# Layer norms with a mean taken from scaled row sums, a residual added by the matmul engine, and a new order of stages

## The chip, the cores and the metric

The kernel runs on one core of a Trainium2 chip. A core has a matmul engine (TensorE, PE in the profile), three engines for elementwise work (VectorE or DVE, ScalarE or ACT, GpSimd or POOL) and a queue that issues transfers (SyncE or SP). The metric is the device time of one execution in microseconds (us), as the median of several runs.

## What is computed

```
h   = q + q_ln * (causal_conv(kv, ssm_k) + kv * ssm_D)     # q_ln = layernorm(q), kv = shift_conv(k) * v
h2  = h + (silu(hn @ w_gate) * (hn @ w_up)) @ w_down       # hn = layernorm(h)
layernorm(x) = (x - mean(x)) / sqrt(var(x) + 1e-5)         # over the last axis, no weights
```

The sequence has 2048 rows, the model width D is 640, the width of the feed-forward part is 1728. All inputs and the output are bfloat16. The long convolution is done in the reference with Fourier transforms; the kernel does it with cosine and sine tables and matmuls.

## The kernel before

The 2048 rows are four blocks of 512 rows. For each block i the kernel runs these stages: `kv` (short convolution of k as matmuls with diagonal matrices, times v, in L551 to L561), `xfwd` (forward transform, L516, evicted by ACT in L522, combined by DVE in L504), `prod` (complex products with the transformed filter, all on DVE, L574 to L587), `ln1` (statistics of the layer norm of q), `inverse` (inverse transform on PE in L617, first residual, second layer norm, a transposing transfer of each quarter into `hnT`), and `ffn` (28 groups of gate and up matmuls in L664 and L665, ACT evictions in L680 and L682, a product on DVE in L684, 112 matmuls of the down projection in L695, the last residual in L703, the store in L706). The filter has its own stages: `ktrans`, `kfwd` and `kcomb`. `prod(i, k)` for k > i adds block i's part of the later blocks' outputs. One buffer each holds `XH`, `kT`, `vT`, `kvo` and `hnT`, so a stage of the next block waits until the last reader of the one before is through. Sixteen `gu` buffers serve the 14 products of an `ffn`, so the gate and up part of the next block can run only two groups ahead of the down projection of the block before.

A layer norm before the change takes four ScalarE passes over a quarter of a block in all: a sum, and a sum of squares of x - mean. Between the two, POOL multiplies the sum by -1/D (L594 for a whole block in `ln1`, L635 for each quarter in `inverse`). After the second, POOL scales and adds epsilon (L600, L639) and takes the power -1/2 (L602, L641), and in `ln1` also multiplies mean and reciprocal root (L604). The normalised q is made by ACT (L624) and multiplied on DVE with the matmul's result in PSUM (L628); L630 adds q. L643 normalises h.

Nothing in the order of instructions is written by hand. Each instruction is a task with a cost, a latency and a priority; `schedule` (L152) simulates the five engines and always gives a free engine the ready task with the lowest priority number, then `emit` (L239) writes one in-order stream for each engine, with semaphore waits. The table `ORDER` (L306) has a number for every engine and stage. The costs are estimates: L594 is planned with 580 ns, L600 with 600 ns, L602 with 650 ns, L604 with 600 ns. An instruction that takes longer on the chip holds up whatever the plan put behind its reader.

Of the kernel before, what the change touches and what calls it, by code (L numbers as in the profile page):

```python
# [64 lines left out]
class _Graph:  # L65
# [37 lines left out]
    def add(self, eng, fn, cost, prio, r=(), w=(), pr=(), pw=(), skip=(), lat=None, nbytes=0, after=()):  # L103
        t = _Task()
        t.eng, t.fn, t.cost, t.prio = eng, fn, cost, prio
        t.lat = lat if lat is not None else {"pe": 200, "act": 110, "dve": 110, "pool": 110, "sp": 2000}[eng]
# [208 lines left out]
    ("dve", "kv2"): 1563.9, ("dve", "kv3"): -223.1, ("dve", "mul"): -299.8, ("dve", "p00"): -640.7,  # L315
    ("dve", "p01"): 1772.6, ("dve", "p02"): 1678.0, ("dve", "p03"): 1641.2, ("dve", "p11"): -646.5,
    ("dve", "p12"): 1612.8, ("dve", "p13"): -299.8, ("dve", "p22"): -853.5, ("dve", "p23"): 1590.2,
    ("dve", "p33"): -216.0, ("dve", "res"): 1564.1, ("dve", "xf0"): -292.2, ("dve", "xf1"): -223.6,
# [13 lines left out]
def bass_sequential_preLN__ssm_conv_h3__swiglu_ffn__prompt_kernel(  # L332
# [39 lines left out]
    with ExitStack() as es:  # L372
# [24 lines left out]
        t1 = sb("t1", 131232, [2, 2, D])  # L397
        t2 = sb("t2", 136352, [2, 2, D])
# [28 lines left out]
        def cpe(n, k):  # L427
            return k * (n / 2.4 + 2.5)

        def cact(n, ptr=0):  # L430
            return 90 + 0.833 * n + 93 * ptr

        def cdve(n):
            return 75 + n / 1.92

        def cps(n):
            return (n + 80) / 0.96
# [87 lines left out]
        def kfwd(m, dst, prio):  # L525
            halves(KT[m], ktab, "kf", dst, KO, 1.0 / N, prio, prio)
# [41 lines left out]
        def prod(j, i, prio):  # L568
            cm, y = C[i - j], Y[i]
            for f2 in range(2):  # L570
# [18 lines left out]
        def ln1(i, prio):  # L589
            x, s = xh[i % 2], st1[i % 2]  # L590
            for j in range(4):
                g.add("act", lambda e, j=j: e.activation(out=qo[j][:], in_=x[:, j, :], func=ACTF.Identity, accum_out=s[:, 0, j:j + 1]),  # L592
                      cact(D, 3), prio, r=[x[:, j, :]], w=[qo[j][:], s[:, 0, j:j + 1]])
            g.add("pool", lambda e: e.tensor_scalar(out=s[:, 1, :], in0=s[:, 0, :], scalar1=-1.0 / D, scalar2=None, op0=ALU.mult), 580, prio,  # L594
                  r=[s[:, 0, :]], w=[s[:, 1, :]])
            for j in range(4):
                g.add("act", lambda e, j=j: e.activation(out=qo[j][:], in_=x[:, j, :], func=ACTF.Square, bias=s[:, 1, j:j + 1],  # L597
                                                         accum_out=s[:, 2, j:j + 1]), cact(D, 4), prio,
                      r=[x[:, j, :], s[:, 1, j:j + 1]], w=[qo[j][:], s[:, 2, j:j + 1]])
            g.add("pool", lambda e: e.tensor_scalar(out=s[:, 3, :], in0=s[:, 2, :], scalar1=1.0 / D, scalar2=LN_EPS, op0=ALU.mult,  # L600
                                                    op1=ALU.add), 600, prio, r=[s[:, 2, :]], w=[s[:, 3, :]])
            g.add("pool", lambda e: e.tensor_tensor(out=s[:, 4, :], in0=s[:, 3, :], in1=half[:, 0:4], op=ALU.pow), 650, prio,  # L602
                  r=[s[:, 3, :], half[:]], w=[s[:, 4, :]])
            g.add("pool", lambda e: e.tensor_tensor(out=s[:, 5, :], in0=s[:, 1, :], in1=s[:, 4, :], op=ALU.mult), 600, prio,  # L604
                  r=[s[:, 1, :], s[:, 4, :]], w=[s[:, 5, :]])

        def inverse(i, prio):
            for j in range(4):
# [14 lines left out]
                q = qo[j % 4]  # L623
# [161 lines left out]
```

## Time and profile before

| what | value |
|---|---|
| median of 3 runs | 312.88 us (312.87 to 313.02) |
| the profiled execution, whole time | 313.7 us |
| its span, first to last instruction | 311.9 us |
| mean granted TensorE clock in it | 0.97 of full speed |
| busy share of the span: PE, DVE, ACT, POOL | 86%, 71%, 56%, 18% |

The shares are averages over stages that differ, so the rows further down cut the span into stretches. In rows of the timeline the columns are the start, the duration, the engine, the line, the operation, what is written and read, the count, and in brackets the idle time of that engine before it and what ended it.

### The profile page before, as it was taken

Reading aid. Unit: us, or ns where it says so; the run is one execution under the profiler, and the core shown is the slowest. Engines: PE = TensorE matmul, PEld = TensorE weight load, DVE = VectorE, ACT = ScalarE, POOL = GpSimd, SP = SyncE. Lnnn points to the kernel's source line nnn. Section 1 sums busy time; section 2 is a strip of 40 time slices with the busy share of each in tenths; the row PEclk is TensorE's granted clock in tenths of the full one; section 3 lists DMA queues with packets and bytes.
Section 4 is the critical chain, followed back from the end, with each engine's and each line's share of the span. In section 5 each row is a group of like instructions: output and inputs, shape, how many; then the busy total and the mean of one; then the engine's idle time right before and its main releaser. Section 6 shows DMA issues by size and latency. Waiting matters only on the chain.

```text
span 311.9 us, 3906 instructions
## 1 busy us (share of the span) xinstructions
PE 268.1 (86%) x1515; PEld 143.6 (46%) x1532; DVE 220.7 (71%) x274; ACT 174.4 (56%) x330; POOL 55.0 (18%) x70
## 2 busy tenths in 40 slices
PE   1988866716865999999999996999999999999995
PEld 1555433402322455545444353665445564544563
DVE  3161899998995799999999699899977431121222
ACT  1759997572826774043288484817779922245400
POOL 0000004073091000023003530540332310000000
PEclk9999999986996999999999997999999999999999
DMA  6999971798405015103403000153000041000011
GB/s 173 249 372 192 208 260 34 142 308 224 86 0 168 0 36 111 47 23 80 130 3 75 10 2 0 38 109 109 0 2 0 18 91 41 1 23 0 0 44 42
DMA packets 55077, 26.92 MB, mean 86 GB/s; under 512 B 45265, under 2 KB 54162, under 8 KB 55058
## 3 DMA queue, kind: packets, MB, share of 16 engines
q1 hardware_dynamic: 55058, 26.67, 33.9%
q8 instruction: 12, 0.20, 0.3%
q14 instruction: 7, 0.06, 0.1%
HBM read 13.49 MB, written 2.62 MB: 52 GB/s over the span
## 4 chain that ended last, share of the span: by engine, by line
PE 45%; DVE 24%; ACT 17%; POOL 10%; issue 2%; DMA 2%; SPq 0%; DVEq 0%
PE ps L695 19%; PE ps L665 9%; PE ps L664 8%; DVE t L576 4%; POOL st L594 3%; PE ps L516 3%; DVE t L574 3%; ACT qo L597 3%; POOL st L600 3%; PE ps L617 3%; DVE XH L504 2%; DVE kT L557 2%; ACT gu L680 2%; ACT KT L494 2%; DVE Y L584 2%
## 5 line engine op out<-in xcount | busy, mean ns | idle before, releaser
L695 PE MATMUL ps<-Wd,gu 128*128 128x320 bf16 x448 | 65.6, 301 | 1.0 <-DVE kT L557 0.6
L680 ACT ACTIVATE gu<-ps 128x512 bf16<-128x512 f32 (+1 forms) x56 | 33.4, 597 | 46.3 <-PE ps L665 42.9
L664 PE MATMUL ps<-hnT,GA 128*128 128x512 bf16 x133 | 52.1, 392 | 6.5 <-ACT ub L682 5.5
L665 PE MATMUL ps<-hnT,UA 128*128 128x512 bf16 x140 | 54.6, 390 | 1.4 <-ACT ub L682 0.5
L695 PEld LDWEIGHTS ps<-Wd,gu 128*128 128x128 bf16 x448 | 41.9, 98 | 24.6 <-issue 6.4
L684 DVE TENSOR_TENSOR gu<-gu,ub 128x512 bf16<-128x512 bf16 (+1 forms) x56 | 23.6, 422 | 34.5 <-ACT ub L682 34.4
L665 PE MATMUL ps<-hnT,UB 128*128 128x512 bf16 x120 | 45.5, 379 | 0.3
L664 PE MATMUL ps<-hnT,GB 128*128 128x512 bf16 x115 | 43.6, 379 | 0.7 <-ACT ub L682 0.7
L682 ACT ACTIVATE ub<-ps 128x512 bf16<-128x512 f32 (+1 forms) x56 | 33.5, 598 | 3.2 <-PE ps L665 2.6
L703 DVE TENSOR_TENSOR xh<-ps,xh 128x640 bf16<-128x640 f32 x16 | 13.2, 823 | 24.1 <-PE ps L695 24.1
L576 DVE TENSOR_TENSOR t<-XH,C 128x2560 bf16<-128x2560 bf16 x20 | 29.8, 1488 | 0.0
L574 DVE TENSOR_TENSOR t<-XH,C 128x2560 bf16<-128x2560 bf16 x20 | 29.7, 1487 | 0.0
L551 PE MATMUL ps<-kT,diag 128*128 128x512 bf16 x76 | 19.5, 406 | 10.6 <-DMA kT<-in_A_k_dram 7.9
L594 POOL TENSOR_SCALAR st<-st 128x4 f32<-128x4 f32 x4 | 11.5, 2865 | 88.7 <-ACT qo L592 88.7
L516 PE MATMUL ps<-KT,ktab 128*128 128x320 bf16 x128 | 21.6, 320 | 5.4 <-ACT KO L522 2.4
L664 PEld LDWEIGHTS ps<-hnT,GA 128*128 128x128 bf16 x140 | 14.0, 100 | 26.2 <-ACT ub L682 7.1
L633 ACT ACTIVATE qo<-xh 128x640 bf16<-128x640 bf16 x16 | 11.7, 734 | 20.0 <-DVE xh L630 20.0
L516 PE MATMUL ps<-kvo,ftab 128*128 128x320 bf16 x128 | 19.8, 300 | 2.2 <-ACT KT L494 1.0
L665 PEld LDWEIGHTS ps<-hnT,UA 128*128 128x128 bf16 x140 | 14.0, 100 | 16.3 <-issue 1.7
L624 ACT ACTIVATE qo<-xh,st 128x640 bf16<-128x640 bf16 x16 | 14.0, 915 | 9.4 <-POOL st L604 9.4
L635 POOL TENSOR_SCALAR mv<-mv 128x1 f32<-128x1 f32 x16 | 5.8, 367 | 74.3 <-ACT qo L633 74.2
L516 PEld LDWEIGHTS ps<-KT,ktab 128*128 128x128 bf16 x128 | 12.2, 104 | 14.1 <-ACT KO L522 3.8
(60 smaller groups left out, 383.9 us busy)
## 6 DMA issues: line engine op xcount, KB each, us to landing
kc<-in_A_ssm_k_dram SPq DMA_DIRECT2D x4, 640.0 KB, 7.1
xh<-in_A_q_dram SPq DMA_DIRECT2D x4, 640.0 KB, 5.3
out_dram<-xh SPq DMA_DIRECT2D x16, 160.0 KB, 1.8
Wd<-in_B_w_down_dram SPq DMA_DIRECT2D x1, 1280.0 KB, 5.8
GA<-in_B_w_gate_dram SPq DMA_DIRECT2D x1, 1120.0 KB, 6.1
UA<-in_B_w_up_dram SPq DMA_DIRECT2D x1, 1120.0 KB, 8.5
GB<-in_B_w_gate_dram SPq DMA_DIRECT2D x1, 960.0 KB, 7.0
UB<-in_B_w_up_dram SPq DMA_DIRECT2D x1, 960.0 KB, 5.4
```

What stands on the lines that cost most here:

```text
L516: last = e.matmul(pt.f(c, W), tab[:, cs, j, f * P:(f + 1) * P], src[:, j, c * W:(c + 1) * W], start=(j == js[0]), stop=(j == js[1]))
L551: last = e.matmul(pt.f(b, N), diag[:, c0 + b, u, :], kT[:, c0 + b, 16 - u:16 - u + N], start=(u == 0), stop=(u == 3))
L574: g.add("dve", lambda e, x=x, k=k: e.tensor_tensor(out=t1[:], in0=x, in1=k, op=ALU.mult), cdve(2560), prio, r=[x, k], w=[t1[:]])
L576: g.add("dve", lambda e, x=x, k=ksw: e.tensor_tensor(out=t2[:], in0=x, in1=k, op=ALU.mult), cdve(2560), prio, r=[x, k], w=[t2[:]])
L594: g.add("pool", lambda e: e.tensor_scalar(out=s[:, 1, :], in0=s[:, 0, :], scalar1=-1.0 / D, scalar2=None, op0=ALU.mult), 580, prio, r=[s[: ...
L624: g.add("act", lambda e, x=x, q=q, s=s, j=j: e.activation(out=q[:], in_=x, func=ACTF.Identity, scale=s[:, 4, j:j + 1], bias=s[:, 5, j:j + ...
L664: e.matmul(pt.f(0, N), wg[:, c, f0:f0 + P], hnT[:, c, :], start=(c == 0), stop=(c == NC5 - 1))
L665: last = e.matmul(pt.f(1, N), wu[:, c, f0:f0 + P], hnT[:, c, :], start=(c == 0), stop=(c == NC5 - 1))
L680: g.add("act", lambda e, pt=pt, gv=gv, a=ps_g: e.activation(out=gv, in_=pt.f(a[0], N, a[1]), func=ACTF.Silu), cact(N), prio, w=[gv], pr=[pt])
L682: g.add("act", lambda e, pt=pt, uv=uv, a=ps_u: e.activation(out=uv, in_=pt.f(a[0], N, a[1]), func=ACTF.Copy), cact(N), prio, w=[uv], pr=[pt])
L684: g.add("dve", lambda e, uv=uv, gv=gv: e.tensor_tensor(out=gv, in0=gv, in1=uv, op=ALU.mult), cdve(N), _Pr("mul", -2), r=[gv, uv], w=[gv])
L695: last = e.matmul(pt.f(c, W), slots[fb][0:k, j * P:(j + 1) * P], Wd[0:k, fb, c * W:(c + 1) * W], start=(fb == 0), stop=(fb == 13))
```

## The change

Four things change together.

1. **Statistics.** ACT's first pass scales by -1/D, so that its accumulated sum is already minus the mean; POOL's multiplication goes (L594, L635), and ACT's second pass waits for ACT's first. POOL adds D times epsilon to the sum of squares and takes the power -1/2, two operations where there were four (`ln1`) or three (`inverse`). The result is too small by the square root of D, which the filter's scale and the evictions of gate and up put right.
2. **First residual branch.** ACT evicts the inverse transform from PSUM with the reciprocal root as its scale; DVE then does (x - mean) times that in one instruction with both tensors in SBUF, where it had multiplied a PSUM tile.
3. **Last residual.** For blocks 0, 1 and 2, two matmuls with the identity put x into each quarter's down projection, and ACT copies the sum out; block 3 keeps DVE's addition.
4. **Order.** Every number of `ORDER` is new, and so are some planned costs and latencies (POOL's in `ln1` 3000 and 1500 ns, in `inverse` 500 and 800 ns). The in-place sums of `prod` go to other halves of the two temporary buffers.

```
-        ... func=ACTF.Identity, accum_out=s[:, 0, j:j + 1])
-        pool tensor_scalar(s[:, 1, :], s[:, 0, :], -1.0 / D, mult)                   580
-        ... func=ACTF.Square, bias=s[:, 1, j:j + 1], accum_out=s[:, 2, j:j + 1])
-        pool tensor_scalar(s[:, 3, :], s[:, 2, :], 1.0 / D, mult, LN_EPS, add)       600
-        pool tensor_tensor(s[:, 4, :], s[:, 3, :], half, pow)                        650
-        pool tensor_tensor(s[:, 5, :], s[:, 1, :], s[:, 4, :], mult)                 600
+        ... func=ACTF.Identity, scale=-1.0 / D, accum_out=s[:, 0, j:j + 1])
+        ... func=ACTF.Square, bias=s[:, 0, j:j + 1], accum_out=s[:, 1, j:j + 1])
+        pool tensor_scalar(s[:, 2, :], s[:, 1, :], LN_EPS * D, add)                  3000
+        pool tensor_tensor(s[:, 3, :], s[:, 2, :], half, pow)                        1500
...
-        act  q = Identity(x, scale=s[:, 4], bias=s[:, 5])
-        dve  q = pt * q                            # pt in PSUM
+        act  q = Copy(pt, scale=s[:, 3])           # pt in PSUM
+        dve  q = (x + s[:, 0]) * q                 # scalar_tensor_tensor
...
+                        if f0 == 0 and onpe:       # onpe = i < RES, RES = 3
+                            for c in range(2):
+                                e.matmul(pt.f(c, W), ident[:], x2[:, c, :], start=True, stop=False)
...
+                if onpe:
+                    act  x2 = Copy(pt)             # priority of ("act", "res")
+                else:
                     dve  x2 = pt + x2
...
 ORDER, some of the entries (before, after; a lower number goes first):
 pe  iv0 -709.4, 740.1   iv1 -135.4, -321.4   kv1 -734.3, 141.5   kf2 -711.2, -40.7   kf3 -644.5, 14.1   ff0 306.1, 622.1
 act iv0 315.3, 697.0    ff0 89.4, 654.1      ln1 52.1, 725.8     kf2 53.1, 814.7     kf3 303.5, 443.3   res -, 425.9
 dve iv0 1585.3, 136.3   kv1 1481.2, 271.9    kc3 1568.2, 504.7   p01 1772.6, 544.8   res 1564.1, 47.2
 sp  kl1 -370.2, 320.2   kl2 -434.3, 206.5    iv0 -412.6, 291.3   kv0 -393.7, 243.7   (weights stay at 45 to 60)
```

## Rows read from the trace of the kernel before

**Rows 1.** The page: busy time by engine, and the granted clock in 40 slices.
```profile
PE 268.1 (86%) x1515; PEld 143.6 (46%) x1532; DVE 220.7 (71%) x274; ACT 174.4 (56%) x330; POOL 55.0 (18%) x70
PEclk9999999986996999999999997999999999999999
```
**Rows 2.** Busy time by stretch: length, busy PE, PEld, DVE, ACT, POOL; clock, DMA.
```profile
0.00:36.50 36.50, 26.50 (x193) 16.91 (x194) 15.43 (x13) 24.52 (x36) 0.40 (x6) 1.00 0.97 241
36.50:80.00 43.50, 26.18 (x147) 12.95 (x148) 41.84 (x46) 30.75 (x60) 13.54 (x17) 0.92 0.71 186
80.00:150.00 70.00, 61.70 (x327) 31.70 (x332) 64.12 (x79) 33.35 (x65) 12.88 (x15) 0.95 0.27 64
150.00:213.40 63.40, 59.34 (x332) 32.29 (x336) 57.25 (x72) 39.20 (x79) 16.91 (x16) 0.97 0.19 45
213.40:312.00 98.60, 94.40 (x520) 49.72 (x524) 42.07 (x67) 46.57 (x94) 11.30 (x16) 0.99 0.09 27
```
**Rows 3.** Timeline of POOL: the statistics of blocks 0, 1 and 2.
```profile
48.22 1.70 POOL L600 TENSOR_SCALAR st<-st 128x4 f32<-128x4 f32 x1 [6.22 <-ACT qo L597]
...
86.35 7.10 POOL L600 TENSOR_SCALAR st<-st 128x4 f32<-128x4 f32 x1 [7.00 <-ACT qo L597]
93.53 1.04 POOL L602 TENSOR_TENSOR st<-st,half 128x4 f32<-128x4 f32 x1
94.66 0.20 POOL L604 TENSOR_TENSOR st<-st 128x4 f32<-128x4 f32 x1
...
169.04 6.54 POOL L594 TENSOR_SCALAR st<-st 128x4 f32<-128x4 f32 x1 [25.07 <-ACT qo L592]
```
**Rows 4.** Timeline of DVE at the ends of those three POOL instructions.
```profile
49.77 1.22 DVE L557 TENSOR_TENSOR kT<-ps,vT 128x1024 bf16<-128x1024 f32 x1
...
96.81 0.43 DVE L684 TENSOR_TENSOR gu<-gu,ub 128x512 bf16<-128x512 bf16 x1 [3.42 <-ACT ub L682]
...
178.49 0.42 DVE L684 TENSOR_TENSOR gu<-gu,ub 128x512 bf16<-128x512 bf16 x1 [3.00 <-ACT ub L682]
```
**Rows 5.** Timeline of ACT: waits for POOL, and rates of back-to-back instructions.
```profile
29.71 2.60 ACT L522 ACTIVATE C<-ps 128x640 bf16<-128x640 f32 x4
51.82 3.36 ACT L624 ACTIVATE qo<-xh,st 128x640 bf16<-128x640 bf16 x4 [1.47 <-POOL st L604]
94.89 0.92 ACT L624 ACTIVATE qo<-xh,st 128x640 bf16<-128x640 bf16 x1 [6.54 <-POOL st L604]
175.61 0.83 ACT L597 ACTIVATE qo<-xh,st 128x640 bf16<-128x640 bf16 x1 [5.33 <-POOL st L594]
```
**Rows 6.** Timeline of PE: start of the first gate group, and idle times behind POOL's stalls.
```profile
79.92 0.38 PE L664 MATMUL ps<-hnT,GA 128*128 128x512 bf16 x1 [0.98 <-issue]
...
96.84 0.61 PE L664 MATMUL ps<-hnT,GA 128*128 128x512 bf16 x1 [5.53 <-ACT ub L682]
...
178.51 0.39 PE L664 MATMUL ps<-hnT,GB 128*128 128x512 bf16 x1 [0.72 <-ACT ub L682]
...
189.98 1.30 PE L617 MATMUL ps<-OS,itab 128*128 128x320 bf16 x8 [2.51 <-DVE OS L504]
```
**Rows 7.** Busy time and clock (third column from the end) just behind two of these idle times.
```profile
96.84:102.30 5.46, 5.46 (x13) 1.93 (x14) 4.37 (x5) 4.32 (x8) 0.00 (x0) 0.50 0.20 69
189.90:195.10 5.20, 5.12 (x24) 2.76 (x24) 4.84 (x8) 0.88 (x2) 0.00 (x0) 0.67 0.00 0
```
**Rows 8.** POOL, second layer norm of block 0: first and last rows of its last 11 instructions.
```profile
63.74 2.05 POOL L639 TENSOR_SCALAR mv<-mv 128x1 f32<-128x1 f32 x1 [2.96 <-ACT qo L637]
...
72.35 1.07 POOL L641 TENSOR_TENSOR mv<-mv,half 128x1 f32<-128x1 f32 x2
```
**Rows 9.** The chain that ended last: start, duration, what.
```profile
247.62 11.93 PE ps L695 x84
```
**Rows 10.** Groups by line and shape: count, busy time and mean of one, idle time before.
```profile
L703 DVE TENSOR_TENSOR xh<-ps,xh 128x640 bf16<-128x640 f32 x16 | 13.2, 823 | 24.1 <-PE ps L695 24.1
L628 DVE TENSOR_TENSOR qo<-ps,qo 128x640 bf16<-128x640 f32 x16 | 13.0, 822 | 1.8 <-PE ps L617 1.0 <-ACT qo L624 0.8
L630 DVE TENSOR_TENSOR xh<-xh,qo 128x640 bf16<-128x640 bf16 x16 | 7.2, 487 | 0.0
```
**Rows 11.** SP's timeline: block 2's load of k, issued behind weight loads; PE's wait for it.
```profile
62.63 6.44 SPq L447 DMA_TRANSPOSE kT<-in_A_k_dram  x1
...
71.64 5.08 PE L551 MATMUL ps<-kT,diag 128*128 128x512 bf16 x15 [7.89 <-DMA kT<-in_A_k_dram]
```

More of the change, by code (lines that the diff above doesn't have):

```diff
@@ L105, in add @@
         t.eng, t.fn, t.cost, t.prio = eng, fn, cost, prio
-        t.lat = lat if lat is not None else {"pe": 200, "act": 110, "dve": 110, "pool": 110, "sp": 2000}[eng]
+        t.lat = lat if lat is not None else {"pe": 200, "act": 190, "dve": 117, "pool": 110, "sp": 2000}[eng]
         t.nbytes = nbytes
@@ L430, in cact @@
         def cact(n, ptr=0):
[L431 removed]
+            return 50 + 0.833 * n + 93 * ptr
         def cdve(n):
[L434 removed]
+            return 69 + n / 1.92
         def cps(n):
[L437 removed]
+            return (n + 65) / 0.96
         def load(dst, src, prio, nbytes, **kw):
@@ L591, in ln1 @@
             for j in range(4):
[L592 to L605, printed above, removed]
+                g.add("act", lambda e, j=j: e.activation(out=qo[j][:], in_=x[:, j, :], func=ACTF.Identity, scale=-1.0 / D,
+                                                         accum_out=s[:, 0, j:j + 1]),
+                      cact(D, 1), prio, r=[x[:, j, :]], w=[qo[j][:], s[:, 0, j:j + 1]])
@@ new lines, in ln1 @@
+                g.add("act", lambda e, j=j: e.activation(out=qo[j][:], in_=x[:, j, :], func=ACTF.Square, bias=s[:, 0, j:j + 1],
+                                                         accum_out=s[:, 1, j:j + 1]), cact(D, 2), prio,
+                      r=[x[:, j, :], s[:, 0, j:j + 1]], w=[qo[j][:], s[:, 1, j:j + 1]])
+            g.add("pool", lambda e: e.tensor_scalar(out=s[:, 2, :], in0=s[:, 1, :], scalar1=LN_EPS * D, scalar2=None, op0=ALU.add), 3000, prio,
+                  r=[s[:, 1, :]], w=[s[:, 2, :]])
@@ L607, in inverse @@
+            g.add("pool", lambda e: e.tensor_tensor(out=s[:, 3, :], in0=s[:, 2, :], in1=half[:, 0:4], op=ALU.pow), 1500, prio,
+                  r=[s[:, 2, :], half[:]], w=[s[:, 3, :]])
         def inverse(i, prio):
@@ L639, in inverse @@
-                g.add("pool", lambda e, m=m: e.tensor_scalar(out=m[:, 2:3], in0=m[:, 2:3], scalar1=1.0 / D, scalar2=LN_EPS, op0=ALU.mult,
-                                                             op1=ALU.add), 600, prio, r=[m[:, 2:3]], w=[m[:, 2:3]])
-                g.add("pool", lambda e, m=m: e.tensor_tensor(out=m[:, 3:4], in0=m[:, 2:3], in1=half[:, 0:1], op=ALU.pow), 650,
+                g.add("act", lambda e, x=x, m=m, q=q: e.activation(out=q[:], in_=x, func=ACTF.Identity, scale=-1.0 / D, accum_out=m[:, 0:1]),
+                      cact(D, 1), prio + 5, r=[x], w=[q[:], m[:, 0:1]])
@@ new lines, in inverse @@
+                g.add("act", lambda e, x=x, m=m, q=q: e.activation(out=q[:], in_=x, func=ACTF.Square, bias=m[:, 0:1], accum_out=m[:, 1:2]),
+                      cact(D, 2), prio + 5, r=[x, m[:, 0:1]], w=[q[:], m[:, 1:2]])
+                g.add("pool", lambda e, m=m: e.tensor_scalar(out=m[:, 2:3], in0=m[:, 1:2], scalar1=LN_EPS * D, scalar2=None, op0=ALU.add), 500,
+                      prio, r=[m[:, 1:2]], w=[m[:, 2:3]])
+                g.add("pool", lambda e, m=m: e.tensor_tensor(out=m[:, 3:4], in0=m[:, 2:3], in1=half[:, 0:1], op=ALU.pow), 800,
@@ L695, in mm @@
                                 last = e.matmul(pt.f(c, W), slots[fb][0:k, j * P:(j + 1) * P], Wd[0:k, fb, c * W:(c + 1) * W],
-                                                start=(fb == 0), stop=(fb == 13))
+                                                start=(fb == 0 and not onpe), stop=(fb == 13))
                         return last
-                    g.add("pe", mm, cpe(W, 2 * (f1 - f0)), prio + 1,
-                          r=[x[0:P, j * P:(j + 1) * P] for x in slots[f0:f1]] + [Wd[:, f0:f1]], pw=[pt])
-                x = xh[i % 2][:, j, :]
-                x2 = x.rearrange("p (b x) -> p b x", b=2)
-                g.add("dve", lambda e, pt=pt, x2=x2: e.tensor_tensor(out=x2, in0=pt.f2(W), in1=x2, op=ALU.add), cps(D), _Pr("res", -2),
-                      r=[x], w=[x], pr=[pt])
+                    g.add("pe", mm, cpe(W, 2 * (f1 - f0) + 2 * (onpe and f0 == 0)), prio + 1,
+                          r=[a[0:P, j * P:(j + 1) * P] for a in slots[f0:f1]] + [Wd[:, f0:f1]] + ([x, ident[:]] if f0 == 0 and onpe else []),
+                          pw=[pt])
+                if onpe:
+                    g.add("act", lambda e, pt=pt, x2=x2: e.activation(out=x2, in_=pt.f2(W), func=ACTF.Copy), cact(D), _Pr("res", -2),
+                          w=[x], pr=[pt])
+                else:
+                    g.add("dve", lambda e, pt=pt, x2=x2: e.tensor_tensor(out=x2, in0=pt.f2(W), in1=x2, op=ALU.add), cps(D), _Pr("res", -2),
+                          r=[x], w=[x], pr=[pt])
                 od = O2[N * i:N * (i + 1), :].rearrange("(p j) d -> p j d", j=4)[:, j, :]
```

68 lines of the change are left out of this document (33 added, 35 removed), and 35 rows, old and new, of the table ORDER.

## The prediction

> **What bounds the kernel now.** I read the busy shares first [rows 1]: PE is busy 86% of the span, far ahead of DVE, but that is an average. So I cut the span where the role changes [rows 2]. Up to 36.5 us PE is busy 26.5 us; from 36.5 to 80 only 26.2 of 43.5 us, while DVE is busy 41.8. From 80 to 150 and from 150 to 213.4 both are near full: PE 61.7 of 70 and 59.3 of 63.4, DVE 64.1 and 57.3. From 213.4 on PE is busy 94.4 of 98.6 us and DVE less than half. So the front is paced by DVE and by the chain to the first gate group at 79.92 us [rows 6], the middle by PE with DVE close behind, and the end by PE alone. In the end nothing but fewer matmuls or an earlier start helps.
>
> Next the idle times of PE behind 80 us [rows 6], traced to their causes. At 91.3 PE stops for 5.53 us: its groups wait for an ACT eviction, and ACT itself stands for 6.54 us at L624 [rows 5], waiting for three POOL instructions of `ln1`, the first of which took 7.10 us [rows 3]. The same instruction took 1.70 us in block 0. What stretches it is seen by setting POOL beside DVE: at 86.35 it starts while DVE runs products back to back, and it ends at 93.45, where DVE's idle time of 3.42 us begins (96.81 - 3.42 = 93.39) [rows 3, 4]. The 6.54 us instruction at 169.04 ends at 175.58, where DVE's 3.00 us of idle time begin (178.49 - 3.00 = 175.49). In block 0 the end at 49.92 lies just behind the start at 49.77 of L557, an instruction that reads PSUM. So POOL comes through when DVE stops or reads PSUM. It is a ring: POOL waits for DVE, ACT for POOL, PE for ACT, and in the end DVE for ACT.
>
> What the ring costs PE: 5.53 us of idle time, and behind it 5.46 us at a granted clock of 0.50 [rows 7], the lower level of 1.2 GHz, so 2.73 us more: 8.26 us. The second stall (ACT 5.33 us at L597 [rows 5]) costs 0.72 us at once. DVE's 3.00 us of idle time push back the inverse of block 2, for which PE waits 2.51 us [rows 6]; then come 5.20 us at 0.67, so 1.72 us: 4.95 us. Together 13.2 us.
>
> **Part 1, the statistics.** L594 and L635 go. The second stall's instruction was an L594, so its 4.95 us have no cause any more: ACT's second pass now waits for ACT's first, on its own engine. Behind that wait stand all evictions queued on ACT; it lasts as long as an accumulator takes to be read and written back, which no row isolates. ACT was idle 44% of the span [rows 1] and the plan may put other work between, so I take nothing and keep 0 to 2 us.
>
> The first stall's instruction, L600, stays (an addition now), with the power behind it. New is what the plan allows: 4.5 us for the two, where the three old ones had 1.85. If the 7.10 + 1.04 us [rows 3] come again, ACT waits 8.1 - 4.5 = 3.6 us; of the old wait PE felt 5.53 of 6.54 us, about 1 us less, so 2.6 us, and the lower clock behind an idle time of about that length cost 1.7 [rows 7]: 4.3 us. No row says whether DVE will be running without a break there. I take half, 2.0 us, between 0 and 8.3 (the old stall whole). So 13.2 us go and 2.0 stay. What is late next once ACT is free is DVE in the middle stretches; it gets its own 6.4 us of idle time back [rows 4] from the same ring.
>
> In `inverse` each quarter has two POOL instructions instead of three. In block 0 the last 11 of 12 ran from 63.74 to 73.42 us [rows 8], 0.88 us each, on the chain to `hnT` and so to the gate group at 79.92. Of these 3 go: 2.6 us earlier. In the later blocks other PE work covers this: nothing.
>
> **Part 2, the first residual branch.** ACT's L624 took 3.36 / 4 = 0.84 us each; an eviction of the same width took 2.60 / 4 = 0.65 [rows 5]. The new one is an eviction with one pointer operand, between these: 0 to 3 us less in all 16, off the path. On DVE, L628 (0.82 us, from PSUM) becomes an instruction with both tensors in SBUF; it is not in the trace. Its bounds are 0.49 (L630, all SBUF) and 0.82 [rows 10]; I take 0.82, as it has two operations, so no change. PSUM is now freed by ACT, and iv has two tiles: a late ACT holds the inverse up, which is in the bounds of the order below.
>
> **Part 3, the last residual.** 12 quarters get two matmuls of 128x320 each: 24 times 11.93 / 84 = 0.142 us [rows 9] is 3.4 us. In the middle and end PE has no slack, so all of it counts. The operand x is final long before, so there is no new wait. DVE loses 12 times 0.82 = 9.9 us [rows 10], ACT gains 12 times 0.65 = 7.8. ACT at 56% takes it: even in the stretch from 150 to 213.4 it was busy 39.2 of 63.4 us [rows 2]. A copy waits behind one or two evictions in ACT's queue, and a second down tile covers that. The last block keeps DVE's addition, so the tail is unchanged.
>
> **Part 4, the order.** On SP the loads of k and v, the transposes of `kvo` and those of `hnT` had numbers below the weights' and now have higher ones, so ready weight loads go first. The load of k for block 2, already behind weight loads, needed 6.44 us to issue and PE waited 7.89 us for it [rows 11]. Later loads of k are covered: their product is read a whole block later. Not covered is a transpose of `hnT` behind the weights, up to the same 6.4 us. On PE and ACT the inverse of block 0 goes from near the front to behind the filter's work. If kf3's eight evictions go first on ACT, that is 8 times 0.65 = 5.2 us later; on DVE it moves forward, past kv1 and most filter sums. PE has some 17 us of idle time between 36.5 and 80 [rows 2]: 7.89 of it is that one wait, which the new order may fill. So the order is worth between -7.9 and +5.2 us (+6.4 if the transposes are caught). I take 0, for want of a row that shows which applies, and count only the 2.6 us of part 1 in the front.
>
> **The sum.** -13.2 + 2.0 - 2.6 + 3.4 = -10.4 us. The profiled execution took 313.7 us (span 311.9 and 1.8 around it), so 303.3; the median of the runs is 0.8 below it, so 302.5.
>
> **Weighed against the skill.** The rows show POOL held while DVE reads only SBUF, and released at an L557 that reads PSUM [rows 3, 4]. The Trainium skill, page "SBUF — State Buffer", section "Who interferes with whom", says that a VectorE instruction with two SBUF inputs blocks a GpSimd instruction that reads SBUF for its whole length, and that one with at most one SBUF input does not. This speaks against the change. By the rule it would make the time that of the third rival.
>
> **The rivals.** First, one stall of the old size stays, because the plan's 4.5 us are too little. Then 8.3 us stand in place of 2.0: 308.8. For it: a stretch of 7.10 us is in the trace; against: one such in four blocks, the others 0.36 to 1.70 or hidden. Second, the order fills the 7.89 us of PE's wait [rows 11] and no stall is left: 312.9 - 13.2 + 3.4 - 7.9 = 295.2. For it: DVE takes the inverse of block 0 early; against: PE and ACT take it late. Third, slower: DVE leaves POOL fewer openings. The 16 instructions of L628 and 12 of the 16 of L703, all reading PSUM [rows 10], leave DVE or turn to SBUF, so POOL's addition is starved in two blocks as it was in block 1, and the shorter chain of block 0 gains nothing: 2 times 8.26 + 3.4 - 13.2 = 6.7, so 319.6. It decides from the point where POOL costs PE more than 13.2 + 2.6 - 3.4 = 12.4 us. For it: every long stretch in the trace lies under products; against: DVE has 9.9 us less to do. Fourth, the parts cancel within 0.6 us of 312.9, the bound under which this kernel's runs can't be told apart.
>
> **How the numbers follow.** The forecast, 297.5 to 306.5 by the bounds of the order and of what is left of the stall: 0.45. First rival, 306.5 to 312.3: 0.20. Second, 290 to 297.5: 0.16. Third, 313.5 to 325: 0.13. Fourth: 0.06. The range leaves out the third and the lower third of the second: 293 to 313. Faster by over 0.2%: 0.45 + 0.20 + 0.16 = 0.81; same 0.06; slower 0.13.
>
> **What would show it.** No wait of ACT's second pass for POOL; ACT's wait for the power under 4 us in each block; PE's idle time behind 80 us below 4 us apart from that, and no stretch at half clock like that from 96.84. The down projection of blocks 0 to 2 longer by 1.1 us each. The first gate group near 77 us. I am wrong if POOL's additions of 5 us or more are waited for in two blocks, if PE stands idle before the first gate group longer than before, or if DVE, with PE waiting for it, becomes the bound of the middle stretch.

## The result, and the profile after

The kernel after took 302.01 us (median of 4 runs, 301.45 to 303.23), the kernel before in the same job 312.95: a ratio of 0.9651, 95% interval 0.9616 to 0.9686. The forecast was 302.5. The profiled execution took 303.23 us with a span of 301.4. In what follows T0 is the start of the first gate group, and "the rest" the time from T0 to the end of the last matmul. Before, they are 79.92 and 228.83 us; after, 83.11 and 215.15. So the rest is 13.7 us shorter and the front 3.2 us longer. The sum was forecast well, its two halves were not: the front had been forecast 2.6 us shorter, the rest 7.8 us shorter (-13.2 + 2.0 + 3.4).

The profiled execution is the slowest of the four of the kernel after, and two executions can differ in T0. The kernel of e6 (below) has the same order of instructions on every engine up to 281 us; its profiled execution reached T0 2.0 us earlier:

```profile
81.13 0.38 PE L658 MATMUL ps<-hnT,GA 128*128 128x512 bf16 x1 [0.24 <-issue]
```

So a difference in T0 of up to 2 us between two traces shows nothing by itself. The rest varies less: in the four kernels with the same order on PE (after, e9, e10, e11) it lies between 215.15 and 215.64 us.

The page of the kernel after, busy time by engine and granted clock of PE in 40 slices, beside [rows 1]:

```profile
PE 269.7 (89%) x1537; PEld 148.3 (49%) x1556; DVE 211.9 (70%) x262; ACT 182.3 (60%) x342; POOL 76.9 (26%) x46
PEclk9999897985699999999999999999999999999999
```

The dips of the clock behind the front are gone, and those in the front are deeper. Busy time by stretch, columns as in [rows 2]:

```profile
0.00:36.50 36.50, 25.46 (x183) 16.56 (x185) 15.63 (x13) 23.80 (x32) 0.40 (x6) 0.99 0.98 240
36.50:83.11 46.61, 31.40 (x156) 16.01 (x156) 43.40 (x47) 31.23 (x63) 10.57 (x10) 0.79 0.70 174
83.11:150.00 66.89, 65.42 (x362) 34.69 (x368) 66.29 (x80) 38.53 (x73) 41.62 (x10) 1.00 0.31 79
150.00:210.00 60.00, 59.68 (x349) 33.60 (x352) 58.69 (x74) 43.73 (x87) 19.90 (x10) 1.00 0.21 45
210.00:298.26 88.26, 87.73 (x494) 47.40 (x498) 27.11 (x50) 45.03 (x91) 4.45 (x10) 1.00 0.09 21
```

From 83.11 us on PE is busy 212.8 of 215.2 us at a granted clock of 1.00. Before, it stood idle for 13.3 us of its rest (228.83 us, 215.52 busy). (19 of the 1556 matmul records of this trace are missing, 15 of them behind T0, so the idle time of 2.3 us is too large rather than too small.) DVE is nearly full from 36.5 to 210 us: 168.4 of 173.5 us. From 36.5 us to T0 PE's clock is 0.79, where it was 0.92 [rows 2]. PE's idle time ahead of T0 is not longer than before (26.3 us against 27.3); its busy time is, 56.9 us for 339 matmuls against 52.6 for 340.

The front in the timelines of PE and of SP (start, duration, what, idle time before and what ended it), beside [rows 6, 11]:

```profile
74.65 2.74 PE L552 MATMUL ps<-kT,diag 128*128 128x512 bf16 x6 [6.99 <-DMA kT<-in_A_k_dram]
...
81.83 1.04 PE L552 MATMUL ps<-kT,diag 128*128 128x512 bf16 x4 [0.97 <-DVE kT L558]
83.11 0.38 PE L658 MATMUL ps<-hnT,GA 128*128 128x512 bf16 x1 [0.24 <-issue]
```

```profile
67.53 4.97 SPq L448 DMA_TRANSPOSE kT<-in_A_k_dram  x1
72.54 0.58 SPq L441 DMA_DIRECT2D UB<-in_B_w_up_dram  x1
73.17 6.41 SPq L448 DMA_TRANSPOSE hnT<-qo  x4
```

The load of k is issued 4.9 us later than before and starts PE's group 3.0 us later. All four transposes of `hnT` stand behind it and a weight load; their issuing ends at 79.58, against 76.12 before, though DVE had finished the last quarter 0.3 us earlier than before (73.56, 73.90).

The statistics on POOL, beside [rows 3], then what DVE did when the longest one ended, then ACT's first reader of the root:

```profile
88.76 33.86 POOL L599 TENSOR_SCALAR st<-st 128x4 f32<-128x4 f32 x1 [16.53 <-ACT qo L596]
122.70 2.25 POOL L601 TENSOR_TENSOR st<-st,half 128x4 f32<-128x4 f32 x1
166.55 10.17 POOL L599 TENSOR_SCALAR st<-st 128x4 f32<-128x4 f32 x1 [26.08 <-ACT qo L596]
...
222.25 0.23 POOL L599 TENSOR_SCALAR st<-st 128x4 f32<-128x4 f32 x1 [24.32 <-ACT qo L596]
```

```profile
121.71 0.81 DVE L582 TENSOR_TENSOR tt<-tt 128x1280 bf16<-128x1280 bf16 x1
122.56 1.49 DVE L585 TENSOR_TENSOR Y<-Y,tt 128x2560 bf16<-128x2560 bf16 x1
```

```profile
126.79 0.80 ACT L622 ACTIVATE qo<-ps,st 128x640 bf16<-128x640 f32 x1 [0.49 <-PE ps L614]
```

An addition that takes 0.23 us in block 3 took 33.86 us in block 1, and ACT did not wait for it: the list of ACT's waits has no line for POOL (18.2 us for the two statistics of `ln1` before). The first reader is L622, which empties the inverse's PSUM at 126.79 and waited for PE, 1.8 us after the power ended at 124.95.

The groups of the new instructions (count, busy time and mean ns of one, idle time before), beside [rows 5, 9, 10]:

```profile
L624 DVE SCALAR_TENSOR_TENSOR qo<-xh,st,qo 128x640 bf16<-128x640 bf16 x16 | 13.6, 876 | 1.6 <-ACT qo L622 1.6
L622 ACT ACTIVATE qo<-ps,st 128x640 bf16<-128x640 f32 x16 | 12.5, 794 | 7.0 <-PE ps L614 7.0
L702 ACT ACTIVATE xh<-ps 128x640 bf16<-128x640 f32 x12 | 8.4, 702 | 28.8 <-PE ps L694 28.8
```

### The profile page after: what moved, and what is told of

It is laid out like the page before. It is cut to its first block, busy times and chain, and to the rows that moved or that the text cites. A ratio compares the mean times of both kernels' runs of the same rounds, so it can differ in the third digit from the quotient of the medians.

```text
span 301.4 us, 3929 instructions
## 1 busy us (share of the span) xinstructions
PE 269.7 (89%) x1537; PEld 148.3 (49%) x1556; DVE 211.9 (70%) x262; ACT 182.3 (60%) x342; POOL 76.9 (26%) x46
## 3 DMA queue, kind: packets, MB, share of 16 engines
HBM read 13.49 MB, written 2.62 MB: 53 GB/s over the span
## 4 chain that ended last, share of the span: by engine, by line
PE 60%; DVE 27%; ACT 7%; POOL 2%; DMA 2%; issue 1%; SPq 0%
PE ps L694 18%; PE ps L659 15%; PE ps L658 13%; PE ps L517 6%; DVE tt L575 5%; DVE tt L577 4%; PE ps L614 3%; ACT KT L495 3%; DVE kT L558 3%; PE ps L552 2%; DVE XH L505 2%; DVE Y L580 2%; DMA kc<-in_A_ssm_k_dram 2%; DVE qo L624 2%; DVE gu L678 2%; DVE Y L582 1%
## 5 line engine op out<-in xcount | busy, mean ns | idle before, releaser
L599 POOL TENSOR_SCALAR st<-st 128x4 f32<-128x4 f32 x4 | 45.7, 11430 | 115.1 <-ACT qo L596 115.1
L659 PE MATMUL ps<-hnT,UA 128*128 128x512 bf16 x140 | 53.1, 379 | 0.8 <-issue 0.6
L658 PE MATMUL ps<-hnT,GA 128*128 128x512 bf16 x133 | 50.4, 379 | 0.2 <-issue 0.2
L552 PE MATMUL ps<-kT,diag 128*128 128x512 bf16 x75 | 22.0, 441 | 10.3 <-DMA kT<-in_A_k_dram 7.0
L575 DVE TENSOR_TENSOR tt<-XH,C 128x2560 bf16<-128x2560 bf16 x20 | 29.7, 1483 | 0.1
L577 DVE TENSOR_TENSOR tt<-XH,C 128x2560 bf16<-128x2560 bf16 x20 | 29.6, 1482 | 0.0
L517 PE MATMUL ps<-kvo,ftab 128*128 128x320 bf16 x128 | 22.2, 323 | 5.4 <-DMA kvo<-kT 3.2
L702 ACT ACTIVATE xh<-ps 128x640 bf16<-128x640 f32 x12 | 8.4, 702 | 28.8 <-PE ps L694 28.8
L658 PEld LDWEIGHTS ps<-hnT,GA 128*128 128x128 bf16 x140 | 13.7, 98 | 17.8 <-issue 1.8
L659 PEld LDWEIGHTS ps<-hnT,UA 128*128 128x128 bf16 x140 | 13.7, 98 | 15.6
L633 POOL TENSOR_SCALAR mv<-mv 128x1 f32<-128x1 f32 x16 | 8.7, 543 | 46.6 <-ACT qo L631 46.6
L517 PEld LDWEIGHTS ps<-kvo,ftab 128*128 128x128 bf16 x128 | 12.8, 104 | 14.3 <-DMA kvo<-kT 4.1
L517 PEld LDWEIGHTS ps<-KT,ktab 128*128 128x128 bf16 x128 | 12.8, 107 | 13.3 <-ACT KO L523 3.2
L552 PEld LDWEIGHTS ps<-kT,diag 128*128 128x128 bf16 x80 | 8.3, 110 | 22.1 <-DMA kT<-in_A_k_dram 7.6
```

The source lines that it names most:

```text
L517: last = e.matmul(pt.f(c, W), tab[:, cs, j, f * P:(f + 1) * P], src[:, j, c * W:(c + 1) * W], start=(j == js[0]), stop=(j == js[1]))
L552: last = e.matmul(pt.f(b, N), diag[:, c0 + b, u, :], kT[:, c0 + b, 16 - u:16 - u + N], start=(u == 0), stop=(u == 3))
L575: g.add("dve", lambda e, x=x, k=k: e.tensor_tensor(out=t1, in0=x, in1=k, op=ALU.mult), cdve(2560), prio, r=[x, k], w=[t1])
L577: g.add("dve", lambda e, x=x, k=ksw: e.tensor_tensor(out=t2, in0=x, in1=k, op=ALU.mult), cdve(2560), prio, r=[x, k], w=[t2])
L599: g.add("pool", lambda e: e.tensor_scalar(out=s[:, 2, :], in0=s[:, 1, :], scalar1=LN_EPS * D, scalar2=None, op0=ALU.add), 3000, prio, r=[s ...
L658: e.matmul(pt.f(0, N), wg[:, c, f0:f0 + P], hnT[:, c, :], start=(c == 0), stop=(c == NC5 - 1))
```

## The experiments

T0 and the rest are read from one profiled execution of each kernel; the ratio is that of the medians to the kernel before on the same chip. The medians of before were 312.9 in the first two jobs, 313.96 for e9 to e11 and 313.15 for e12, so ratios are compared.

| kernel | median us | ratio, 95% interval | T0 | the rest |
|---|---|---|---|---|
| before | 312.95 | 1 | 79.92 | 228.83 |
| after | 302.01 | 0.9651 [0.9616, 0.9686] | 83.11 | 215.15 |
| e1 new arithmetic, old order | 305.98 | 0.9772 [0.9753, 0.9790] | 81.56 | 219.77 |
| e2 old arithmetic, new order | 317.50 | 1.0145 [1.0115, 1.0174] | 84.78 | 228.75 |
| e3 before, statistics on DVE | 303.42 | 0.9698 [0.9683, 0.9712] | 79.55 | 218.84 |
| e4 after, statistics on DVE | 306.97 | 0.9790 [0.9738, 0.9842] | 85.38 | 217.08 |
| e5 after, no residual on PE | 303.98 | 0.9708 [0.9686, 0.9731] | 83.14 | 216.17 |
| e6 after, residual on PE in all four | 303.64 | 0.9692 [0.9662, 0.9721] | 81.13 | 216.32 |
| e7 load of k behind `hnT` | 320.10 | 1.0228 [1.0191, 1.0265] | 75.93 | 238.94 |
| e8 early reader of the root | 309.50 | 0.9886 [0.9863, 0.9908] | 86.20 | 217.92 |
| e9 weights behind `hnT` | 303.69 | 0.9677 [0.9647, 0.9707] | 83.26 | 215.49 |
| e10 memset between products | 302.68 | 0.9666 [0.9621, 0.9711] | 81.44 | 215.26 |
| e11 less accumulation on DVE | 302.29 | 0.9645 [0.9604, 0.9685] | 83.48 | 215.64 |
| e12 e9, evictions of k ahead on DVE | 303.87 | 0.9694 [0.9659, 0.9729] | 76.96 | 220.91 |

### The arithmetic and the order, each alone (e1, e2)

e1 is the kernel after with the numbers, costs and latencies of the plan before; e2 is the kernel before, in its arithmetic, with those of after.

```
e1  -    ("pe", "iv0"): 740.1, ... ("sp", "kl2"): 206.5, ...    # the whole table and the costs
    +    ("pe", "iv0"): -709.4, ... ("sp", "kl2"): -434.3, ...
e2  the other way round
```

> The changed kernel's statements (statistics, first residual branch, last residual of blocks 0 to 2 by the identity) with the priority table, costs and latencies of the kernel before. Theory A (the gain is the waits of ScalarE for GpSimd, which the new statements take out because the reciprocal root is read only when the inverse transform is evicted): 301 to 305 us, and ScalarE's waits for GpSimd in ln1 and inverse under 1 us in all. Theory B (the gain is the new order of stages): 309 us or more.

> The statements of the kernel before with the new priority table, latencies and costs (3000 ns for both scalings and 1500 ns for the power in ln1). Theory A: ScalarE stands behind GpSimd again, for 5 us or more in at least one block, and the time is 308 us or more. Theory B: 301 to 305 us.

e1 came out 1 us above the range of its theory A, e2 within the range of its own. The arithmetic alone gives 6.9 us, the order alone costs 4.6, both together give 10.9: the order is worth 4 us, but only with the new arithmetic. In e2 POOL and the transfers are still waited for (ACT waits 4.3 us for the root once, not the 5 us expected). Its timeline of POOL, then of PE:

```profile
95.59 9.19 POOL L599 TENSOR_SCALAR st<-st 128x4 f32<-128x4 f32 x1 [11.95 <-ACT qo L596]
```

```profile
108.16 0.61 PE L663 MATMUL ps<-hnT,GB 128*128 128x512 bf16 x1 [3.25 <-ACT ub L681]
...
157.86 0.61 PE L663 MATMUL ps<-hnT,GA 128*128 128x512 bf16 x1 [6.13 <-DMA hnT<-qo]
```

Its rest is that of before to 0.1 us, so all that the new order did there was to move T0 4.9 us back. In e1 the rest is 9.1 us shorter; T0 is 1.6 us later, which is within what T0 varies by. POOL's addition took as long there as in after, and ACT waited for POOL nowhere behind T0:

```profile
86.04 36.44 POOL L600 TENSOR_SCALAR st<-st 128x4 f32<-128x4 f32 x1 [11.70 <-ACT qo L597]
```

### What the ring costs (e3, e4)

In the kernel before, the instructions of `ln1` that stood on POOL run on DVE at the same place of the plan; in the kernel after the same.

```
+    for t in self.glob:
+        if t in self.moved:          # ln1's POOL instructions; the power becomes a product
+            t.eng = "dve"
```

> The kernel before with its plan kept, but the four small instructions of ln1 in each block run on VectorE at the place that the plan gives them in time (left out: the power -1/2, in whose place a multiplication stands). If the waits for a starved GpSimd cost what was read from the trace, 13.2 us go and some 2 us of small VectorE work come: 300 to 303 us. If they hid other waits that now come last, 307 us or more.

> The changed kernel with its plan kept and the two small instructions of ln1 on VectorE (left out: the power -1/2, a multiplication stands in its place). GpSimd's addition took 33.9 us in block 1, but nobody waits for it by the trace. Theory A: no change, 301 to 303 us. The rival (the starved GpSimd still delays the inverse transforms): 295 to 299 us.

Without POOL in `ln1` the kernel before is 9.5 us faster (303.42, just above the 300 to 303 expected), and its rest is 10.0 us shorter. That is less than the ring cost, because the move makes a wait of its own. At the start of block 0's `ffn`, ACT's second pass over block 1 waits for the moved first instruction, which stands on DVE behind two products. ACT's evictions come later by that, and PE waits 3.01 us for one. ACT, DVE and PE in e3, then ACT at the same instruction in the kernel before:

```profile
82.85 0.83 ACT L606 ACTIVATE qo<-xh,st 128x640 bf16<-128x640 bf16 x1 [3.33 <-DVE st L603]
82.66 0.16 DVE L603 TENSOR_SCALAR st<-st 128x4 f32<-128x4 f32 x1
87.03 0.39 PE L673 MATMUL ps<-hnT,GA 128*128 128x512 bf16 x1 [3.01 <-ACT ub L691]
```

```profile
79.39 0.83 ACT L597 ACTIVATE qo<-xh,st 128x640 bf16<-128x640 bf16 x1 [0.35 <-POOL st L594]
```

The wait of 5.53 us that PE had at 91.3 [rows 6] is gone in e3: from 87.03 to 200 us no wait of PE is longer than 0.7 us. Behind the wait of 3.01 us PE's clock is low; busy time and clock of e3 there:

```profile
87.03:92.00 4.97, 4.75 (x15) 1.94 (x17) 4.05 (x10) 3.69 (x9) 0.00 (x0) 0.66 0.00 0
```

That is 3.01 + 0.34 * 4.97 = 4.7 us that the kernel before did not have. So the ring cost at least 10.0 us of the rest, and 14.7 by an estimate that takes these 4.7 us out.

The kernel after with the same move is 5 us slower, where neither theory had put it. T0 is 2.3 us later, little more than T0 varies by (ahead of it DVE's small instruction waits 0.70 us for ACT in DVE's own queue). The rest is 1.9 us longer, but PE's idle time in it is not (1.9 us): the first 2.62 us behind T0 have a granted clock of 0.50, the next 4.00 us one of 0.79, which costs 2.1 us. So taking POOL out of `ln1` gains nothing there. That is what a cause looks like that was there before and is not there any more, though POOL is starved longer than ever.

### Why a starved POOL no longer costs (e8, e10)

e8 adds to the kernel after one small ACT instruction for each block, which reads the root as soon as the plan has it. e10 adds a DVE memset, which reads no SBUF, ahead of every second product.

```
e8   +  act  st[5] = Copy(st[3])            # placed where the plan has the power's end
e10  +  dve  memset(128x8 f32)              # 20 of them
        dve  tt = XH * C                    # second product
```

> The changed kernel with its plan kept and one small ScalarE instruction more for each block (128x4, it copies the reciprocal roots to a spare place), put where the plan has them ready. Theory A (GpSimd's 34 us cost nothing only because no ScalarE instruction reads the result before the inverse transform): ScalarE stands for 4 us or more in block 1 and in another, PE with it, 308 us or more. Rival (the starved GpSimd does no harm in this order): 301.5 to 304 us.

> The kernel after with its plan kept, and one DVE memset of 128x8 f32 ahead of each second product of the filters and convolutions, 20 in all: an instruction that reads no SBUF, between two that each read two SBUF tensors. The question is what lets POOL's addition L599 through, which took 33.86 us in block 1 and 10.17 in block 2 of the kernel after while DVE ran products back to back (alone it takes 0.2). Theory A, POOL is let in whenever DVE runs an instruction without two SBUF inputs, however short: the longest addition on POOL falls below 6 us (two products and an accumulation lie between two memsets). Theory B, only a gap in which DVE is empty lets it in, and a short memset leaves none: it stays above 8 us. In both the time is that of after plus some of 20 times a short instruction on DVE: 301.5 to 304 us, since nothing waits for POOL in the kernel after. The Trainium skill, page SBUF - State Buffer, section Who interferes with whom, would give theory A.

With the early reader 7.5 us come back. Its ACT waits:

```profile
54.52 0.20 ACT L618 ACTIVATE st<-st 128x4 f32<-128x4 f32 x1 [5.08 <-POOL st L616]
...
178.94 0.20 ACT L618 ACTIVATE st<-st 128x4 f32<-128x4 f32 x1 [5.46 <-POOL st L616]
```

The waits came in blocks 0 and 2. In block 1, where one was expected, the addition took only 0.94 us in this run. The first wait lies ahead of T0, which is 3.1 us later; the rest is 2.8 us longer. So the distance between the power and its reader is what made the starvation harmless.

With the memsets (65 ns each) the starvation is gone. POOL in e10, then what DVE did when these three additions ended:

```profile
47.06 1.23 POOL L603 TENSOR_SCALAR st<-st 128x4 f32<-128x4 f32 x1 [46.14 <-ACT qo L600]
...
87.17 0.78 POOL L603 TENSOR_SCALAR st<-st 128x4 f32<-128x4 f32 x1 [16.62 <-ACT qo L600]
...
164.96 0.63 POOL L603 TENSOR_SCALAR st<-st 128x4 f32<-128x4 f32 x1 [26.09 <-ACT qo L600]
```

```profile
46.72 1.48 DVE L579 TENSOR_TENSOR tt<-XH,C 128x2560 bf16<-128x2560 bf16 x1
...
86.38 1.48 DVE L579 TENSOR_TENSOR tt<-XH,C 128x2560 bf16<-128x2560 bf16 x1
...
164.66 0.83 DVE L584 TENSOR_TENSOR tt<-tt 128x1280 bf16<-128x1280 bf16 x1
```

33.86 us became 0.78 and 10.17 became 0.63, and the time did not change. With e8 this says that in the kernel after nothing hangs on POOL. Theory A's number came out (all below 6 us), but not by its mechanism: none of the three additions ended at a memset. Each ended 0.09 us behind the end of the DVE instruction under which it had begun, which has two SBUF inputs and is followed by the next one without a gap. Why POOL is let in there, and not between such instructions in the kernel after, no run shows.

The Trainium skill, page "SBUF — State Buffer", section "Who interferes with whom", says that a VectorE instruction with two SBUF inputs holds a GpSimd instruction that reads SBUF, and that one with at most one SBUF input, outside the two-port modes, does not. The additions of e10 agree with the first part; the 33.86 us in the kernel after are longer than any one DVE instruction there (1.49 us).

A gap lets POOL in as well. In the kernel after, from 86 to 124 us, each row of DVE starts before the row ahead of it ends, except one: L585 at 122.56, 0.04 us behind L582, and POOL's addition ended at 122.62. In block 2 the only such place, 0.03 us at 176.65, is where the addition of 166.55 ended (176.72). All traces agree: of the 23 POOL instructions over 3 us in the fourteen kernels, 16 ended less than 0.1 us behind the start of the first gap of DVE, and the other 7 0.17 to 0.18 us behind the start of the first product that reads PSUM. So it hangs on a gap of some 0.05 us whether POOL starves: in e5, e8, e9 and e11 a gap of 0.07 or 0.08 us let the addition of block 1 in after 0.93 or 0.94 us, with no memset. What e10 shows therefore rests on all three blocks together.

### The residual on PE (e5, e6)

```
-    RES = 3
+    RES = 0          # e6: RES = 4
```

> The changed kernel with the last residual on VectorE in all four blocks (no identity matmuls), same priority table. If PE alone sets the time behind the first gate group (it is idle for 2.3 of 215 us there), the 24 matmuls less give 3.4 us: 298 to 300 us. Rival: VectorE, busy for 66.3 of the 66.9 us from 83.1 to 150, is the other bound, and the 9.9 us that come back to it make PE wait: 303 us or more.

> The changed kernel with the last residual by the identity in all four blocks. 8 matmuls more on PE at the end, where PE is never idle: 1.1 us more, and an eviction by ScalarE in place of VectorE's addition behind the last matmul, 0.1 us less: 303 us. Rival: no difference that can be measured, if the planner's order shifts by as much: 301 to 302.5 us.

The rival held. Taking 24 matmuls away made the rest 1.0 us longer and the time 2 us (the intervals of the ratios just touch). Between 83.14 and 150 us, and the two waits of PE that make up most of its idle time there:

```profile
83.14:150.00 66.86, 63.23 (x348) 33.05 (x347) 66.11 (x82) 32.77 (x63) 7.78 (x10) 0.99 0.30 71
```

```profile
135.91 1.04 PE L552 MATMUL ps<-kT,diag 128*128 128x512 bf16 x4 [1.83 <-DVE kT L558]
146.59 0.39 PE L658 MATMUL ps<-hnT,GA 128*128 128x512 bf16 x1 [1.47 <-DMA hnT<-qo]
```

PE is idle for 3.6 us where the kernel after has 1.5, and DVE is full. With the residual of the last block on PE as well (e6), the rest is 1.2 us longer, as the eight matmuls would make it (1.1 us by the prediction's price); in the time it can't be told from the kernel after.

### What holds T0, and what an earlier T0 brings (e7, e9, e11, e12)

e7 plans block 2's load of k behind block 0's transposes. The plan is made anew with this condition. e9 keeps the plan of the kernel after and moves four weight loads on SP behind these transposes. e11 cuts DVE's accumulating additions short. e12 is e9 with DVE's three products with v (L558 in after), which empty the PSUM of block 2's k, ahead of six products.

```
e7   tload(kT[:], ..., after=(hn_done[0:4] if i == 2 else ()))
e9   g.behind([GB, UB, Wd, Wd], hn_done[0:4])     # on SP only
e11  tensor_tensor(yy[..., 0:64], yy[..., 0:64], tacc[..., 0:64], add)
e12  e9, and six products of prod(0, 1) behind kv(2)'s products with v, on DVE only
```

> The changed kernel with block 2's load of k planned behind the four transposes into hnT of block 0 (it is issued 5 us ahead of them in the changed kernel, and PE does block 2's short convolution ahead of the first gate group). If the queue of SyncE sets the first gate group at 83.1 us, that group comes at 78 to 80 us and the time is 297 to 300 us. Rival: VectorE is full from 36.5 to 150 us either way, PE then waits for its products by as much, and the time is 301 to 303 us.

> The kernel after with its plan kept, but five weight loads (GB, UB, two of Wd) stand on SP just behind block 0's four transposes of hnT, instead of ahead of block 2's load of k and of these transposes. In the kernel after the first gate group starts at 83.11 us, the transposes of hnT are issued at 73.17 us behind the load of k (67.53 to 72.54) although their first operand was ready at 69.14, and PE waits 6.99 us for that load. Theory A, SP's queue and its transfers set the front: the load of k is issued and lands 3 to 5 us earlier, the transposes follow, the gate group starts at 78 to 80, and the end comes as much earlier: 297 to 300 us. Theory B, DVE is full from 36 to 150 us and sets the whole stretch: the gate group may come earlier, but PE waits for DVE behind it by the same amount (idle behind the gate group 5 us or more instead of 2.3), and the time is 301 to 303.5 us. The moved loads may also come too late for the products that read them; then PE waits for a DMA of GB, UB or Wd, which the list of waits would show.

> The kernel after with its plan kept, and the accumulating additions of the convolution on DVE cut to 64 of the 640 columns (the rest of the accumulation is left out), which takes about 15 us of busy time off DVE, most of it between 36 and 210 us. Theory A, PE alone sets the end behind the first gate group (it stands idle 2.3 us of 215): the time falls by no more than 2.3 us plus what the front gains, and the front waits for transfers: 299.5 to 302. Theory B, DVE sets the front, from 36 to 83 us, where it is busy 43.4 of 46.6 us: the gate group comes 3 us or more earlier, and the time is 296 to 299 us.

> The kernel of e9 (weights behind block 0's transposes of hnT), and on DVE the three products with v that empty the PSUM of block 2's k go ahead of the first six products of the next convolution; nothing else is moved. In e9 the load of k landed at 69.1 us instead of 74.65, but PE then waited 6.09 us for these three, which stood at 80.29 to 84.65 behind products, and the first gate group stayed at 83.26. Theory A, the first gate group sets the time, and it was DVE's place for these three that held it: the gate group starts at 78 to 80.5 us (then held by the transposes of hnT), what comes behind keeps its length of about 215 us, and the time is 298 to 300.5. Theory B, what is pushed back on DVE (six products, about 5 us) comes back as waits of PE for DVE behind the gate group: the gate group is as early, PE's idle time behind it grows from 2 us to 5 or more, and the time is 301.5 to 304.

None of the theories of e7 and e9 came out as a whole. In e9 the load of k lands 5.5 us earlier, and T0 does not move. PE in e9, then DVE:

```profile
69.10 2.74 PE L558 MATMUL ps<-kT,diag 128*128 128x512 bf16 x6 [5.63 <-DMA kT<-in_A_k_dram]
...
81.57 1.89 PE L558 MATMUL ps<-kT,diag 128*128 128x512 bf16 x4 [6.09 <-DVE kT L564]
```

```profile
80.29 2.35 DVE L564 TENSOR_TENSOR kT<-ps,vT 128x1024 bf16<-128x1024 f32 x2
```

PE's wait moved from the transfer to DVE, where these two stand behind products that the plan put first. e12 puts them first, and T0 falls by 6.2 us against after. PE in e12, and its busy time from there to 150:

```profile
69.09 6.15 PE L569 MATMUL ps<-kT,diag 128*128 128x512 bf16 x16 [5.83 <-DMA kT<-in_A_k_dram]
75.68 1.04 PE L569 MATMUL ps<-kT,diag 128*128 128x512 bf16 x4 [0.44 <-DVE kT L575]
76.96 0.38 PE L678 MATMUL ps<-hnT,GA 128*128 128x512 bf16 x1 [0.24 <-issue]
...
88.33 0.39 PE L678 MATMUL ps<-hnT,GA 128*128 128x512 bf16 x1 [1.46 <-ACT ub L696]
...
99.73 0.72 PE L533 MATMUL ps<-kvo,ftab 128*128 128x320 bf16 x4 [1.42 <-ACT XH L539]
```

```profile
76.96:150.00 73.04, 67.11 (x369) 34.43 (x370) 72.44 (x86) 38.57 (x72) 47.74 (x10) 1.00 0.42 110
```

The rest grows by 5.8 us, and the time does not fall: the median is 1.9 us above that of after, with intervals that overlap. DVE is busy 72.44 of 73.04 us, and PE stands idle for 5.9 us where after has 1.5. In the two waits for ACT, ACT itself had waited for DVE, 2.33 us at 87.67 and 2.21 us at 98.97. So theory B held. (4.5 of the 5.8 us are this idle time; the remainder can't be split, for the missing matmul records.) In e7 the front was emptied further and it went worse: T0 at 75.93, the rest 23.8 us longer. Twenty matmuls of block 2's short convolution moved behind T0, PE stands idle there for 12.4 us, and its clock is 0.97. The longest wait is 4.65 us for ACT at 97.52, where ACT had waited 6.23 us for DVE's products. As the whole plan changed, these parts are not told apart.

e11 has 12 us less on DVE and gains nothing: PE fills the rest (215.64 us). All of the 12 us lie behind 110 us, where the accumulating additions begin; from 36.5 to 83.1 DVE is busy 43.32 us in e11 and 43.39 in after. So its theory B, DVE as the bound of the front, was not tested. Together these fit two bounds that meet: the rest has a floor near 215.2 us, which is PE's own work (no kernel here is below it), and DVE's work up to 150 us sets how early that stretch can end. The first is borne out by e11, the second is only argued, from e12. A kernel with less DVE work ahead of T0 was not run, nor one with that and an earlier T0, and no kernel here is faster than the kernel after beyond the intervals.

## Why the prediction came out as it did

- **The ring, -13.2 us.** The mechanism was right, and the size lies within what e3 allows: at least 10.0 us, and 14.7 without the wait that e3 makes itself.
- **What is left of the stall, +2.0 us.** The step that failed is "ACT waits 8.1 - 4.5 = 3.6 us". It compared POOL's delay with the planned 4.5 us, and the delay was far larger than the 8.1 us taken, 33.86 + 2.25 us. But ACT waited 0, so the term is 0. The reader had changed with part 2: before, L624 needed the root early to normalise q; now L622 needs it when the inverse is in PSUM, 38 us after the addition started. The text had described that edit under "Part 2" and not carried it over to part 1. e8 shows the price of an early reader.
- **The third rival** was right that POOL would be starved in two blocks (in this trace), and wrong that it would cost: "2 times 8.26" is the price of a stall that PE had felt, taken over without asking which instruction would read the root.
- **The shorter chain of block 0, -2.6 us.** POOL's chain is shorter: 8 instructions in 7.17 us in place of 11 in 9.68 (2.5 us less). It began 1.3 us later, the last quarter was ready only 0.3 us earlier, and T0 did not hang on it: what was late next was the queue on SP, and behind it DVE's place for the products with v (e9, e12). The prediction named the danger for the transposes and priced it at up to 6.4 us; it did happen, and the load of k as well came later.
- **The order, 0 us.** It was priced for the front only. There it cost 4.9 us with the old arithmetic, and with the new 1.6, no more than T0 varies by. Behind T0 it gave nothing with the old and 4.6 us with the new. No bound covered that gain: the text took parts 1 and 4 as independent terms.
- **The identity matmuls, +3.4 us.** 24 of them do take what was said: a pair starts 0.27 us before the next matmul (119.93 to 120.20 us), 12 pairs 3.2 us. But the rest is 1.0 us shorter with them (e5), as DVE, nearly full, no longer has the 9.9 us. The step that failed is "In the middle and end PE has no slack, so all of it counts": without them PE waits for DVE and for a transfer there, 1.83 and 1.47 us in e5 against 0.95 us for DVE in the kernel after.
- **The prices** of single instructions were near: STT 0.88 us for 0.82, ACT's eviction 0.79 for 0.65 to 0.84, ACT's copy 0.70 for 0.65.
- **The signs named.** No wait of ACT for POOL: right. PE's idle time behind T0 under 4 us: right, 2.3. No stretch at half clock behind T0: right. Down projection 1.1 us longer: right. PE idle ahead of T0 for longer, as a sign of being wrong: did not come, 26.3 us against 27.3. T0 near 77: wrong, 83.11 (81.13 in e6's execution). DVE as the bound of the middle: not so in the kernel after, but PE waits for it as soon as T0 comes earlier (e12) or DVE keeps the residual (e5).

So the total was close by luck: two errors of about 6 us cancelled, the front 5.8 us too early (3.8 by e6's execution), the rest 5.9 us too long. The 5.9 us are nearly the two terms that were added for the rest, +2.0 for a stall that did not come and +3.4 where -1.0 was measured, 6.4 us. The -13.7 of the rest can't be split further: the ring is bounded only from 10.0 to 14.7, and the terms are not independent, as with the old order the whole arithmetic shortens the rest by 9.1 (e1). Of PE's 13.3 us of idle time behind T0 the prediction had counted 8.8; the small waits that make up the others went too, and no run isolates them.

## What to carry to other kernels

Price a slow helper by the wait of its first reader, not by its own time; an edit that moves the reader may be worth more than one that shortens the helper. When an order is changed, ask for its worth under both versions of the work, and look at each queue that it moves things past: a front that waits for a transfer may be held by another engine's queue right behind. Before an instruction is moved to another engine to see what its wait costs, look at what it will wait for in the new queue. Where two engines are full in the same stretch, a wait taken from one can come back as a wait for the other, as in e12.

## What was not expected of the hardware

- A POOL addition on 128x4 values took from 0.23 to 39.99 us (e12, block 1) by what DVE did beside it. It ended where DVE's rows show a gap as small as 0.03 us, and with one 65 ns memset of DVE for each product pair it stayed below 1.3 us.
- Idle time in the front costs PE twice. Behind waits of 3.21 us (at 65.77) and 6.99 us (at 74.65) the granted clock in the stretch 65.00 to 83.10 was 0.62, between the levels of 1.2 and 2.4 GHz. Fifteen matmuls of the short convolution took 2.74 + 3.25 us there, and 3.41 us in the next block, at 1.00:

```profile
77.61 3.25 PE L552 MATMUL ps<-kT,diag 128*128 128x512 bf16 x9 [0.22 <-issue]
...
130.07 3.41 PE L552 MATMUL ps<-kT,diag 128*128 128x512 bf16 x15
```
